# Float64 weights converted and split on VectorE, combinations 1024 columns at a time and in three phases

## The chip, the cores and the metric

The kernel runs on one core of a Trainium2 chip. The metric is the device time of one execution in microseconds (us); lower is better. The kernel before took 1769.65 us (median of three runs, 1762.01 to 1774.15).

## What is computed

Two attentions in a row for each of 8 batches and 8 heads (32 packed queries read 576 tokens; the tokens then read the packed result), and behind them two feed-forward layers over 4608 tokens, with 512 features at the ends and 2048 in the middle. All inputs come as 8-byte floats in the layout that the kernel reads as pairs of 32-bit words.

```python
def attn(q, k, v, p):
    packed = sm_attn(p, k, v)
    return sm_attn(q, packed, packed)
x = attn(q, k, v, p).transpose(0, 2, 1, 3).reshape(4608, 512)
h = x @ w_in                      # first up product
x = (h * cos(h)) @ w_out          # first down product
h = x @ w_in2                     # second up product
g = where(h >= 1, h, where(h <= -1, 0, (h + 1) ** 2 / 4))
out = g @ w_out2                  # second down product
```

## The kernel before, in words

Every operand of a large matmul is held as two parts, `hi` and `lo`, made by `split` (L66 to L69): ScalarE copies the source into the rounded `hi`, and another engine subtracts it from the source to give `lo`. Three matmuls (`TERMS`) stand for one product. That other engine is GpSimd unless a call names VectorE. The weights arrive as float64 and are made float32 by `convert` (L124 to L139): ScalarE scales the high words, VectorE does four integer and multiply operations (L131, L132, L135, L136), and GpSimd adds the two parts (L139).

The program runs in stages. Stage one is attention together with the first up product, where the attention's second half is folded into a matrix `M = packed @ w_in` per batch. A list of items `(n, hf, fp)` (L970 on) gives the order: batch `n`, half `hf` of its tokens, pair `fp` of feature tiles. `up` (L591) does 12 matmuls into `hps`, and `u`, a copy out of PSUM, goes to `h1T` in DRAM. Between two items, `step` advances side streams that are Python generators: `mat` and `load` make M (`form_M`, `load_M`: a product in `psB`, a copy `cp`, a turn through a DMA into `ml`, a split into `m`), `att` does attention, `wt` and `wo` convert weights. `cut_w_in` and `cut_w_out` make the weights of the first layer in 16 pieces of 128 x 512 each. `cut_w_out` is started at batch B - 2, and each item advances it by one step, two steps a piece; at `n == B - 1`, half 1, everything still open is drained in program order.

`combine` (L525) prepares the second layer's weights. The second up and down products use seven products in place of eight, in the manner of Strassen and Winograd, and so need sums of weight blocks. One unit converts four blocks of 128 x 256, two at a time, forms four sums, splits seven blocks in four calls (tile `pl`) and stores them to `su` or `sd` in DRAM. Eight units for the up weights run in stage one behind batch 2, eight for the down weights in the second up product.

Stage two, `run_down1`, is the first down product: 128 turns, each with 24 matmuls, an activation on ScalarE and VectorE (`act_a`, `act_b`) and a split into `r` on VectorE. Stage three, `run_up2`, is the second up product: seven products of 12 matmuls for each pair of feature tiles, their sums out of PSUM on VectorE (L708), an activation ending in L716, and the `ty` operands with differences and splits on GpSimd. `step("wt")` stands behind each product whose name does not begin with Z. Stage four, `run_down2`, is the second down product.

A tile scheduler sets the final order on each engine from program order, priorities and a model of times. `behind(last_act)` puts an instruction after the latest `u` copy of ScalarE.

## Time and profile before

| what | us |
|---|---|
| median of three runs | 1769.65 |
| lowest, highest | 1762.01, 1774.15 |
| the profiled execution | 1761.84 |
| its span, first to last instruction | 1759.9 |

Over the span TensorE is busy 90%, its weight loads 86%, VectorE 69%, ScalarE 53%, GpSimd 30%; the mean granted clock is 0.942 of full speed. In the profile, PE is TensorE, DVE VectorE, ACT ScalarE, POOL GpSimd. Matmuls are pipelined, so TensorE can count as busy without being at its rate; for that, matmul counts are set against time. The shares are averages over stages with different limits, so a stretch of the span is read by itself.

### The profile page before, as it was taken

Reading aid. Unit: us, or ns where it says so; the run is one execution under the profiler, and the core shown is the slowest. Engines: PE = TensorE matmul, PEld = TensorE weight load, DVE = VectorE, ACT = ScalarE, POOL = GpSimd, SP = SyncE. Lnnn points to the kernel's source line nnn. Section 1 sums busy time; section 2 is a strip of 40 time slices with the busy share of each in tenths; the row PEclk is TensorE's granted clock in tenths of the full one; section 3 lists DMA queues with packets and bytes.
Section 4 is the critical chain, followed back from the end, with each engine's and each line's share of the span. In section 5 each row is a group of like instructions: output and inputs, shape, how many; then the busy total and the mean of one; then the engine's idle time right before and its main releaser. Section 6 shows DMA issues by size and latency. Waiting matters only on the chain. (4 is left out here: it accounts for less than half of the span.)

```text
span 1759.9 us, 28596 instructions
## 1 busy us (share of the span) xinstructions
PE 1584.2 (90%) x10846; PEld 1514.2 (86%) x10846; DVE 1210.4 (69%) x1675; ACT 930.8 (53%) x1514; POOL 519.6 (30%) x376
## 2 busy tenths in 40 slices
PE   8679899897670999999999898998999899999998
PEld 6469688795560999999999888988999899999998
DVE  4883257455776887777776478888666597778775
ACT  3343344443333766666666367676766444444443
POOL 2863255565664010000001265556533000000000
PEclk7789799998975999999999999999999899999999
DMA  6566788988867444344342756565436954444430
GB/s 229 163 204 230 208 287 276 311 288 253 271 226 250 134 143 120 109 122 118 106 122 92 269 193 212 196 230 173 177 135 226 378 168 135 129 135 135 135 109 34
DMA packets 174538, 326.95 MB, mean 186 GB/s; under 512 B 16192, under 2 KB 70464, under 8 KB 170816
## 3 DMA queue, kind: packets, MB, share of 16 engines
q1 hardware_dynamic: 120128, 230.73, 42.6%
q10 hardware_dynamic: 54272, 94.39, 14.5%
q8 instruction: 85, 1.39, 0.3%
q14 instruction: 53, 0.43, 0.1%
HBM read 184.55 MB, written 130.02 MB: 179 GB/s over the span
## 5 line engine op out<-in xcount | busy, mean ns | idle before, releaser
L602 PE MATMUL hps<-at,m 128*128 128x288 f32 x1536 | 243.6, 313 | 42.1 <-ACT at L67 15.3
L602 PEld LDWEIGHTS hps<-at,m 128*128 128x128 f32 x1536 | 223.8, 199 | 59.0 <-ACT at L67 17.1
L67 ACT ACTIVATE r<-g 128x576 fp32r<-128x576 f32 x224 | 153.7, 687 | 184.6 <-PE psZ L909 72.6
L68 DVE TENSOR_TENSOR r<-g,r 128x576 fp32r<-128x576 f32 x224 | 166.3, 754 | 71.1 <-ACT r L67 71.1
L807 PE MATMUL psZ<-r,wo 128*128 128x288 f32 x1536 | 206.1, 296 | 0.0
L807 PEld LDWEIGHTS psZ<-r,wo 128*128 128x128 f32 x1536 | 205.2, 188 | 0.0
L68 POOL TENSOR_TENSOR ty<-td,ty 128x576 fp32r<-128x576 f32 x32 | 52.2, 1644 | 382.9 <-ACT ty L67 382.9
L68 DVE TENSOR_TENSOR r<-t,r 128x576 fp32r<-128x576 f32 x128 | 99.8, 779 | 95.0 <-ACT r L67 94.9
L909 PE MATMUL psZ<-r,sw 128*128 128x288 f32 x1152 | 159.6, 298 | 3.7 <-DVE r L68 2.8
L909 PEld LDWEIGHTS psZ<-r,sw 128*128 128x128 f32 x1152 | 156.5, 190 | 4.2 <-DVE r L68 3.0
L807 PE MATMUL psX<-r,wo 128*128 128x288 f32 x768 | 124.3, 297 | 37.9 <-ACT r L67 37.7
L716 DVE SCALAR_TENSOR_TENSOR t<-hh,t 128x576 f32<-128x576 f32 x128 | 123.9, 969 | 48.1 <-ACT t L715 48.0
L807 PEld LDWEIGHTS psX<-r,wo 128*128 128x128 f32 x768 | 110.1, 189 | 38.5 <-ACT r L67 38.0
L67 ACT ACTIVATE r<-t 128x576 fp32r<-128x576 f32 x128 | 87.8, 686 | 101.5 <-PE psZ L807 52.4
L714 ACT ACTIVATE t<-hh,half 128x576 f32<-128x576 f32 x128 | 98.5, 771 | 57.3 <-DVE hh L708 40.1
L807 PE MATMUL psY<-r,wo 128*128 128x288 f32 x768 | 123.9, 297 | 0.0
L730 PE MATMUL psZ<-ty,sw 128*128 128x288 f32 x768 | 113.9, 299 | 8.5 <-DVE hh L708 8.3
L730 PEld LDWEIGHTS psZ<-ty,sw 128*128 128x128 f32 x768 | 106.6, 190 | 10.1 <-DVE hh L708 9.8
L909 PE MATMUL psX<-r,sm 128*128 128x288 f32 x768 | 108.5, 301 | 7.3 <-ACT r L67 6.2
L909 PEld LDWEIGHTS psX<-r,sm 128*128 128x128 f32 x768 | 105.6, 192 | 8.5 <-ACT r L67 6.5
L807 PEld LDWEIGHTS psY<-r,wo 128*128 128x128 f32 x768 | 110.1, 189 | 0.0
L773 DVE SCALAR_TENSOR_TENSOR t<-h,t 128x576 f32<-128x576 f32 x128 | 99.0, 774 | 14.5 <-ACT t L772 5.4
(160 smaller groups left out, 3066.4 us busy)
## 6 DMA issues: line engine op xcount, KB each, us to landing
h1T<-u ACTq DMA_DIRECT2D x128, 288.0 KB, 3.5
h<-h1T SPq DMA_DIRECT2D x128, 288.0 KB, 2.8
gT<-t ACTq DMA_DIRECT2D x128, 288.0 KB, 2.3
g<-gT SPq DMA_DIRECT2D x128, 288.0 KB, 3.2
raw<-in_moe_w_in SPq DMA_DIRECT2D x32, 512.0 KB, 5.7
raw<-in_moe_w_out SPq DMA_DIRECT2D x32, 512.0 KB, 4.7
su<-pl SPq DMA_DIRECT2D x56, 256.0 KB, 4.4
sd<-pl SPq DMA_DIRECT2D x56, 256.0 KB, 3.0
```

The source lines that it names most:

```text
L67: nc.scalar.activation(out=hi, in_=src, func=AF.Copy)
L68: (eng or nc.gpsimd).tensor_tensor(out=lo, in0=src, in1=hi.bitcast(F32), op=ALU.subtract)
L602: nc.tensor.matmul(out=hps[:, j, :HB], lhsT=m[:, w, G, cs], rhs=x[:, G, y], start=(G == 0 and i == 0), stop=(G == 1 and i == 2),)
L714: nc.scalar.activation(out=t, in_=h, func=AF.Relu, scale=0.5, bias=half)
L716: nc.vector.scalar_tensor_tensor(out=t, in0=h, scalar=1.0, in1=t, op0=ALU.max, op1=ALU.min)
L730: nc.tensor.matmul(out=ps[:, i], lhsT=s[:, d, w, cs], rhs=t[:, d, y], start=first and d == n == 0, stop=d == 1 and n == 2, skip_group_chec ...
L773: nc.vector.scalar_tensor_tensor(out=t, in0=G1[i], scalar=1 / (2 * PI), in1=ki, op0=ALU.mult, op1=ALU.subtract)
L807: nc.tensor.matmul(out=acc[d // 2][:, d % 2], lhsT=wo[f // 4, w][:, f % 4, ds], rhs=r[:, y, k], start=f == n == 0, stop=f == NFT - 1 and n ...
L909: nc.tensor.matmul(out=ps[:, j], lhsT=s[:, f % 4, w, j * 128:j * 128 + 128], rhs=r[:, y, k], start=first and f == n == 0, stop=f == 7 and ...
```

## The change

`convert` adds its two parts on VectorE. All splits of weights (`w_in`, `w_out`, `pl`) and of M name VectorE. `cut_w_in` loads two pieces ahead, with three buffers. `combine` loads and converts a unit's four blocks in one piece of 1024 columns, puts the sums into the first half of the raw tile, and has no `slow`. Half of the down weights' units move into `run_down1`, one step every four turns, and are drained at turn 104; the other half stay in `run_up2`, where a step stands behind products X1 and X2 alone. `cut_w_out` starts half a batch (eight items) earlier. Splits and differences of attention (`at`, `mt`, `x`) and of `ty` stay on GpSimd.

```diff
@@ convert
-        nc.gpsimd.tensor_tensor(out=a, in0=a, in1=lf, op=ALU.add)
+        nc.vector.tensor_tensor(out=a, in0=a, in1=lf, op=ALU.add)
@@ cut_w_in (from_f64 and w_in_rows go)
+        def load(hp):
+            raw = stg.tile([128, 512, 2], I32, tag="raw", name="raw", bufs=3)
...
+        raws = [load(hp) for hp in range(2)]
+        for hp in range(4):
+            if hp % 2 == 0:
+                t = wpool.tile([128, 2, 2, 512], F32R, tag="w", name="wi")
+            a = stg.tile([128, 512], F32, tag="w32", name="w32", bufs=2)
+            convert(raws[hp], a)
+            if hp < 2:
+                raws.append(load(hp + 2))
+            yield
+            split(t[:, hp % 2, 0], t[:, hp % 2, 1], a, nc.vector)
@@ form_M, load_M, cut_w_out
-                split(t[:, 0, G], t[:, 1, G], a)
+                split(t[:, 0, G], t[:, 1, G], a, nc.vector)
...
-            split(t[:, 0, G], t[:, 1, G], halves[G])
+            split(t[:, 0, G], t[:, 1, G], halves[G], nc.vector)
...
-                split(wo[f // 4, 0][:, f % 4], wo[f // 4, 1][:, f % 4], a)
+                split(wo[f // 4, 0][:, f % 4], wo[f // 4, 1][:, f % 4], a, nc.vector)
@@ combine
-    def combine(units, slow):
-        def load(src, x):
-            raw = prep[0].tile([128, 2, 256, 2], I32, tag="raw", name="raw", bufs=2)
-            nc.sync.dma_start(out=raw, in_=src(x))
+    def combine(units):
+        def load(src):
+            raw = prep[0].tile([128, 4, 256, 2], I32, tag="raw", name="raw")
+            for x in range(2):
+                nc.sync.dma_start(out=raw[:, 2 * x:2 * x + 2], in_=src(x))
...
-            for raw, o in zip(raws, (slice(0, 4, 3), slice(1, 3))):
-                convert(raw, a[:, o], last_act)
-                yield
-                store()
-            s = prep[0].tile([128, 4, 256], F32, tag="raw", name="pc", bufs=2)
+            convert(raw, a, last_act)
+            store()
+            yield
+            s = raw[:, :2].bitcast(F32).rearrange("p m c t -> p (m c t)").rearrange("p (k c) -> p k c", c=256)
...
-                    split(hl[:, 0, :n], hl[:, 1, :n], x)
+                    split(hl[:, 0, :n], hl[:, 1, :n], x, nc.vector)
...
-                if k < 5:
-                    for _ in range(slow - 1):
-                        yield
...
+            if u + 1 < len(units):
+                raw = load(units[u + 1][0])
+                yield
@@ run_down1
+        prep[:] = [pd.enter_context(tc.tile_pool(name="prep1", bufs=1, reuse_waits="tile"))]
+        streams["wt"].append(combine(list(units_down())[:4]))
...
+            if i % 4 == 2:
+                step("wt")
             if i == 13 * 8:
+                drain("wt")
@@ run_up2
-        last_act.clear()
-        streams["wt"].append(combine(units_down(), 2))
+        streams["wt"].append(combine(list(units_down())[4:]))
...
-                    if o[0] != "Z":
+                    if o[0] == "X":
                         step("wt")
@@ items
-            streams["wt"].append(combine(units_up(), 2))
-        if n == B - 2 and fp == 0 and hf == 0:
+            streams["wt"].append(combine(units_up()))
+        if n == B - 3 and fp == 0 and hf == 1:
             streams["wo"].append(cut_w_out())
```

Line numbers move: L131 to L139 of before are L134 to L142 after, L609 is L604, L773 and L781 are L770 and L778.

The first place is VectorE at the end of stage one, from its last `u` copy on; `w` is a converted piece of `w_out`, `wo` its split tile. Before:

```order
L609 COPY u<-hps 128x576
L131 TENSOR_SCALAR w_4597<-raw 128x512
L132 SCALAR_TENSOR_TENSOR w_4597<-raw,w_4597 128x512
L135 TENSOR_SCALAR raw<-w_4597 128x512
L136 SCALAR_TENSOR_TENSOR raw<-raw 128x512
L131 TENSOR_SCALAR w_4610<-raw 128x512
L132 SCALAR_TENSOR_TENSOR w_4610<-raw,w_4610 128x512
L135 TENSOR_SCALAR raw<-w_4610 128x512
L136 SCALAR_TENSOR_TENSOR raw<-raw 128x512
L131 TENSOR_SCALAR w_4621<-raw 128x512
```

After:

```order
L604 COPY u<-hps 128x576
L68 TENSOR_TENSOR wo<-w_4461,wo 128x512
L134 TENSOR_SCALAR w_4509<-raw 128x512
L135 SCALAR_TENSOR_TENSOR w_4509<-raw,w_4509 128x512
L138 TENSOR_SCALAR raw<-w_4509 128x512
L139 SCALAR_TENSOR_TENSOR raw<-raw 128x512
L142 TENSOR_TENSOR w_4509<-w_4509,raw 128x512
L68 TENSOR_TENSOR wo<-w_4509,wo 128x512
L68 TENSOR_TENSOR pl<-raw,pl 128x512
L134 TENSOR_SCALAR w_4552<-raw 128x512
L135 SCALAR_TENSOR_TENSOR w_4552<-raw,w_4552 128x512
L138 TENSOR_SCALAR raw<-w_4552 128x512
```

Before, two conversions more follow these, then L773 of stage two, and their five splits stand on GpSimd. After, the rest of one conversion and two splits follow, then L770.

The second place is VectorE in the first turns of stage two, where `t` and `r` are the stage's own tiles and `h` its input. Before:

```order
L68 TENSOR_TENSOR r_4870<-t,r_4870 128x576
L773 SCALAR_TENSOR_TENSOR t<-h_4671,t 128x576
L68 TENSOR_TENSOR r_4904<-t,r_4904 128x576
L781 TENSOR_TENSOR t<-h_4669,t 128x576
L773 SCALAR_TENSOR_TENSOR t<-h_4673,t 128x576
L781 TENSOR_TENSOR t<-h_4671,t 128x576
L773 SCALAR_TENSOR_TENSOR t<-h_4834,t 128x576
L68 TENSOR_TENSOR r_4938<-t,r_4938 128x576
L781 TENSOR_TENSOR t<-h_4673,t 128x576
```

After:

```order
L778 TENSOR_TENSOR t<-h_4605,t 128x576
L134 TENSOR_SCALAR pa<-raw 128x1024
L770 SCALAR_TENSOR_TENSOR t<-h_4609,t 128x576
L778 TENSOR_TENSOR t<-h_4607,t 128x576
L135 SCALAR_TENSOR_TENSOR pa<-raw,pa 128x1024
L770 SCALAR_TENSOR_TENSOR t<-h_4773,t 128x576
L68 TENSOR_TENSOR r_4880<-t,r_4880 128x576
L778 TENSOR_TENSOR t<-h_4609,t 128x576
L138 TENSOR_SCALAR raw<-pa 128x1024
L68 TENSOR_TENSOR r_4914<-t,r_4914 128x576
L778 TENSOR_TENSOR t<-h_4773,t 128x576
```

The 1024-column operations on `pa` and `raw` are those of the first unit of `combine`; they now stand one by one between those of the stage.

The third place is where M is split, late in stage one: before, on GpSimd, where `m` is M's split tile, `ml` its source and `pl` that of `combine`.

```order
L68 TENSOR_TENSOR wo<-w_3913,wo 128x512
L68 TENSOR_TENSOR m<-ml,m 128x512 x3
L139 TENSOR_TENSOR pa<-pa,raw 128x2x256
L139 TENSOR_TENSOR w_4013<-w_4013,raw 128x512
L68 TENSOR_TENSOR m<-ml,m 128x512
L139 TENSOR_TENSOR pa<-pa,raw 128x512
L68 TENSOR_TENSOR m<-ml,m 128x512
L68 TENSOR_TENSOR wo<-w_4013,wo 128x512
L350 TENSOR_TENSOR x<-x,mx_4232 128x1152
L68 TENSOR_TENSOR m<-ml,m 128x512
L68 TENSOR_TENSOR pl<-pa,pl 128x512
```

After, on VectorE, in the same part of the program:

```order
L68 TENSOR_TENSOR m<-ml,m 128x512
L68 TENSOR_TENSOR wo<-w_3645,wo 128x512
L68 TENSOR_TENSOR wo<-w_3701,wo 128x512
L453 COPY cp<-psB 128x512
L134 TENSOR_SCALAR w_3772<-raw 128x512
L378 STREAM_TRANSPOSE a_3857<-x 128x576
L135 SCALAR_TENSOR_TENSOR w_3772<-raw,w_3772 128x512
L138 TENSOR_SCALAR raw<-w_3772 128x512
L139 SCALAR_TENSOR_TENSOR raw<-raw 128x512
L142 TENSOR_TENSOR w_3772<-w_3772,raw 128x512
L134 TENSOR_SCALAR pa<-raw 128x1024
L68 TENSOR_TENSOR wo<-w_3772,wo 128x512
```

The splits of M have moved into the queue in which `cp`, the copies out of `psB`, and the conversions stand.

## Rows read from the trace of the kernel before

**Rows 1.** The table of stretches, all engines; columns named in its first line
```profile
core 0: us, PE busy (x) PEld busy (x) DVE busy (x) ACT busy (x) POOL busy (x), PEclk, DMA share, GB/s
0.00:130.00 130.00, 97.10 (x399) 75.81 (x400) 90.03 (x131) 53.88 (x114) 78.04 (x63) 0.76 0.63 198
130.00:400.00 270.00, 249.31 (x1520) 220.04 (x1518) 136.07 (x232) 112.40 (x238) 124.78 (x100) 0.96 0.81 266
400.00:533.00 133.00, 89.17 (x482) 77.85 (x481) 89.40 (x113) 49.70 (x85) 85.06 (x63) 0.83 0.80 258
533.00:570.60 37.60, 0.02 (x1) 0.02 (x1) 25.27 (x32) 14.72 (x23) 18.53 (x14) 0.55 0.66 228
570.60:982.20 411.60, 411.37 (x3072) 411.02 (x3073) 291.77 (x394) 268.90 (x399) 17.48 (x11) 1.00 0.43 128
982.20:1226.90 244.70, 219.34 (x1539) 213.50 (x1537) 197.35 (x253) 158.31 (x252) 140.80 (x91) 0.96 0.60 203
1226.90:1366.30 139.40, 139.40 (x1046) 139.40 (x1047) 93.28 (x118) 99.24 (x151) 54.88 (x34) 1.00 0.49 183
1366.30:1417.00 50.70, 40.66 (x268) 39.17 (x267) 32.02 (x47) 24.71 (x38) 0.00 (x0) 0.87 0.89 346
```

**Rows 2.** TensorE's timeline: start us, us, instruction, count [idle before, releaser]
```profile
488.47 1.09 PE L602 MATMUL hps<-at,m 128*128 128x288 f32 x3 [14.13 <-ACT at L67]
...
531.00 1.88 PE L602 MATMUL hps<-at,m 128*128 128x288 f32 x12 [2.05 <-ACT u L611]
570.58 0.61 PE L807 MATMUL psX<-r,wo 128*128 128x288 f32 x1 [37.70 <-ACT r L67]
...
956.60 25.76 PE L807 MATMUL psZ<-r,wo 128*128 128x288 f32 x192
```

**Rows 3.** VectorE's timeline, 440 to 580, the same columns
```profile
471.38 2.35 DVE L552 TENSOR_TENSOR pc<-pa 128x256 f32<-128x256 f32 x1
...
508.28 0.41 DVE L552 TENSOR_TENSOR pc<-pa 128x256 f32<-128x256 f32 x1
...
543.93 0.69 DVE L132 SCALAR_TENSOR_TENSOR w<-raw,w 128x512 int32<-128x512 int32 x1
544.66 0.43 DVE L135 TENSOR_SCALAR raw<-w 128x512 int32<-128x512 int32 x1
...
548.23 1.37 DVE L135 TENSOR_SCALAR raw<-w 128x512 int32<-128x512 int32 x1
```

**Rows 4.** GpSimd's timeline, 500 to 580, the same columns
```profile
537.86 1.39 POOL L68 TENSOR_TENSOR wo<-w,wo 128x512 fp32r<-128x512 f32 x1 [0.74 <-ACT wo L67]
...
547.92 1.39 POOL L68 TENSOR_TENSOR wo<-w,wo 128x512 fp32r<-128x512 f32 x1 [0.74 <-ACT wo L67]
...
562.40 1.26 POOL L68 TENSOR_TENSOR wo<-w,wo 128x512 fp32r<-128x512 f32 x1 [0.74 <-ACT wo L67]
```

**Rows 5.** ScalarE's timeline, 455 to 580; ACTq is its queue of issues
```profile
472.47 8.20 ACTq L86 DMA_DIRECT2D h1T<-u  x2
480.77 0.65 ACT L611 ACTIVATE u<-hps 128x576 f32<-128x576 f32 x1 [8.33 <-DVE u L609]
...
561.70 0.63 ACT L67 ACTIVATE wo<-w 128x512 fp32r<-128x512 f32 x1 [3.40 <-POOL w L139]
564.65 1.41 ACT L772 ACTIVATE t<-h 128x576 int32<-128x576 f32 x2 [2.32 <-DMA h<-h1T]
```

**Rows 6.** Groups by line and shape, whole span: busy us, mean ns, idle before, releasers
```profile
L716 DVE SCALAR_TENSOR_TENSOR t<-hh,t 128x576 f32<-128x576 f32 x128 | 123.9, 969 | 48.1 <-ACT t L715 48.0
...
L68 DVE TENSOR_TENSOR r<-t,r 128x576 fp32r<-128x576 f32 x128 | 99.8, 779 | 95.0 <-ACT r L67 94.9
L773 DVE SCALAR_TENSOR_TENSOR t<-h,t 128x576 f32<-128x576 f32 x128 | 99.0, 774 | 14.5 <-ACT t L772 5.4
...
L68 POOL TENSOR_TENSOR m<-ml,m 128x512 fp32r<-128x512 f32 x64 | 87.2, 1373 | 67.0 <-ACT m L67 52.8 <-DVE x L343 4.9 <-DMA raw<-in_moe_w_out 3.9
```

**Rows 7.** Who TensorE waited for, 0 to 533: total us, times, longest us
```profile
PE psB L449 <- ACT cp L455: 20.3, 12, 4.8
```

More of the change, by code (lines that the diff above doesn't have):

```diff
@@ L122, in drain, with words @@
             pass
+    def words(src):
+        return src.bitcast(I32)
     def convert(raw, a, after=()):
@@ L391, in new_M @@
         ready.add(("new", n, c))
-    def from_f64(src, dst):
-        raw = stg.tile([128, 512, 2], I32, tag="raw", name="raw", bufs=2)
-        nc.sync.dma_start(out=raw, in_=words(src).rearrange("p (c t) -> p c t", t=2))
-        a = stg.tile([128, 512], F32, tag="w32", name="w32", bufs=2)
-        convert(raw, a)
-        yield
-        split(dst[:, 0], dst[:, 1], a)
-    def w_in_rows(c, hp):
-        return w_in[hp * 128:(hp + 1) * 128, c * 512:(c + 1) * 512]
     WI = {}
     def cut_w_in(c):
-        for i in range(2):
-            t = wpool.tile([128, 2, 2, 512], F32R, tag="w", name="wi")
-            for j in range(2):
-                yield from from_f64(w_in_rows(c, 2 * i + j), t[:, j])
-                WI[c, 2 * i + j] = t[:, j]
-                ready.add(("wi", c, 2 * i + j))
-                yield
+        def load(hp):
+            raw = stg.tile([128, 512, 2], I32, tag="raw", name="raw", bufs=3)
+            src = words(w_in[hp * 128:(hp + 1) * 128, c * 512:(c + 1) * 512])
+            nc.sync.dma_start(out=raw, in_=src.rearrange("p (c t) -> p c t", t=2))
+            return raw
+        raws = [load(hp) for hp in range(2)]
[8 more added lines that the diff above has]
+            split(t[:, hp % 2, 0], t[:, hp % 2, 1], a, nc.vector)
+            WI[c, hp] = t[:, hp % 2]
+            ready.add(("wi", c, hp))
+            yield
     def form_M(g, c):
@@ L538, in combine @@
         units = list(units)
-        raws = [load(units[0][0], x) for x in range(2)]
+        raw = load(units[0][0])
         yield
         for u, (_, dst) in enumerate(units):
-            following = units[u + 1][0] if u + 1 < len(units) else None
             a = prep[0].tile([128, 4, 256], F32, tag="pa", name="pa")
-            for raw, o in zip(raws, (slice(0, 4, 3), slice(1, 3))):
-                convert(raw, a[:, o], last_act)
-                yield
-                store()
-            s = prep[0].tile([128, 4, 256], F32, tag="raw", name="pc", bufs=2)
-            raws = [load(following, 0)] if following else []
+            convert(raw, a, last_act)
+            store()
+            yield
+            s = raw[:, :2].bitcast(F32).rearrange("p m c t -> p (m c t)").rearrange("p (k c) -> p k c", c=256)
             tt = nc.vector.tensor_tensor
-            tt(out=s[:, 0], in0=a[:, 3], in1=a[:, 2], op=ALU.add)
-            tt(out=s[:, 2], in0=a[:, 0], in1=a[:, 3], op=ALU.subtract)
+            tt(out=s[:, 0], in0=a[:, 1], in1=a[:, 3], op=ALU.add)
+            tt(out=s[:, 2], in0=a[:, 0], in1=a[:, 1], op=ALU.subtract)
             tt(out=s[:, 1], in0=s[:, 0], in1=a[:, 0], op=ALU.subtract)
-            tt(out=s[:, 3], in0=a[:, 1], in1=s[:, 1], op=ALU.subtract)
+            tt(out=s[:, 3], in0=a[:, 2], in1=s[:, 1], op=ALU.subtract)
             yield
@@ L557, in combine @@
                 hl = prep[0].tile([128, 2, 2, 256], F32R, tag="pl", name="pl")
[L558 removed]
+                x = {0: a[:, 0:4:2], 2: a[:, 3:4], 3: s[:, :2], 5: s[:, 2:]}[k]
                 with behind(last_act):
[L560 removed]
+                    split(hl[:, 0, :n], hl[:, 1, :n], x, nc.vector)
                 for i in range(n):
@@ L564, in combine @@
                 store()
-                if k < 5:
-                    for _ in range(slow - 1):
-                        yield
-            if following:
-                raws.append(load(following, 1))
-            yield
-        store()
+            if u + 1 < len(units):
+                raw = load(units[u + 1][0])
+                yield
     def units_up():
```

3 lines of the change are left out of this document (removed).

## Prediction

> **What bounds the kernel now.** Read the table of stretches first [rows 1], then TensorE's timeline for the places where it stands still [rows 2], then what VectorE, GpSimd and ScalarE do there [rows 3 to 5], then the groups by line [rows 6]. In the table the reader is to compare matmul counts with time. At full rate TensorE runs 192 matmuls in 25.76 us [rows 2], that is 0.1333 us each.
>
> Four stages. (a) Attention and the first up product end at 570.6, where the first L807 matmul starts after 37.70 us of idleness [rows 2]. (b) The first down product, 570.6 to 982.2: 3072 x 0.1333 = 409.6 of 411.6 us, so TensorE alone sets it. (c) The second up product: 1539 x 0.1333 = 205.2 of 244.7 us up to 1226.9, 39.5 lost; then 1046 x 0.1333 = 139.4 of 139.4, nothing lost. The lossy part is the part in which combine runs. (d) The handover to the second down product, 1366.3 to 1417: 268 matmuls, 35.7 of 50.7 us, 15 lost [rows 1]. Stage (a) is far from the rate nearly everywhere: TensorE is busy 97.1 of 130 us at a mean clock of 0.76, 249.3 of 270, and 89.2 of 133 at 0.83, which mixes 2.4 and 1.2 GHz [rows 1]. No engine is full there; chains are what lasts: a result goes from ScalarE to GpSimd or from VectorE to GpSimd and back before a weight can be used.
>
> A second thing is to be seen in rows 3 and 4. The same VectorE operation has two prices. L135 takes 0.43 us at 544.66, with GpSimd idle, and 1.37 at 548.23, beside GpSimd's 1.39 us split at 547.92. L552 takes 0.41 at 508.28 and 2.35 at 471.38. In the groups L716 has a mean of 969 ns, L773, the same shape in a stage with hardly any GpSimd work, 774 [rows 6]. So work that leaves GpSimd also makes VectorE's own work shorter.
>
> **The change, part by part.** Prices on VectorE alone: 0.41 us for 256 columns, 0.69 for 512 with two inputs, 0.43 for 512 with one [rows 3]. From 0.41 and 0.69 each further 256 columns cost 0.28, so 1024 columns are estimated at 1.25; the one-input form at 0.86 at most.
>
> Load of VectorE in stage (a). Added: 64 splits of M, 32 splits and 32 sums of weights, 512 columns each, 128 x 0.69 = 88 us; for eight units of combine a sum of 1.25, three splits of 0.69 and one of 0.41, 8 x 3.7 = 30. It is busy 90.0 + 136.1 + 89.4 + 25.3 = 341 of 570.6 us now [rows 1]. 341 + 118 = 459 is 80%, before anything is given back by GpSimd falling silent. So it does not become the bound on average.
>
> (1) End of stage (a). After TensorE's last first-up matmul (531.00 + 1.88) six w_out tiles are still split on GpSimd, at 537.86 to 562.40, 4.9 us apart ((562.40 - 537.86) / 5) [rows 4]; then ScalarE has its last wo at 561.70, waits for h1 until 564.65 [rows 5], and the first matmul comes at 570.58. In the order of the changed kernel the stream starts eight items earlier and behind the last u copy stand three splits and two conversions, where four conversions (five splits) stood. Two tiles less: 2 x 4.9 = 9.8. The other three lose a GpSimd sum and split of about 1.39 each [rows 4] for 0.69 each on VectorE: 3 x 1.4 = 4.2, and one transfer between engines each. I take -15. Bounds: -28 (37.70 less the 8.9 us from the last wo to the first matmul, which nothing here removes) and +5 (VectorE's three splits wait for ScalarE one by one).
>
> (2) The chain to the last batch. At 488.47 TensorE has waited 14.13 us for the split attention of the last batch [rows 2]. ScalarE stood for 8.20 us at the issue of an h1T store that needs a u copy of VectorE [rows 5], and VectorE's work in front of that copy was stretched, as L552 with 2.35 us for 0.41 [rows 3]. I take half of the 14.13, -7; bounds -14 and +10 (this stretch now holds more VectorE work).
>
> (3) Start and M. A split of M on GpSimd takes 1373 ns on the mean [rows 6], on VectorE 0.69. TensorE's largest wait up to 533 is 20.3 us on ScalarE's copies out of psB [rows 7]; that in-order engine holds splits that wait for GpSimd's sums. I take half, -10; bounds -30 (the same gain in the other waits of the start) and +15.
>
> (4) Second up product. A unit of combine has eleven steps now, four steps per pair of feature tiles, and such a pair takes TensorE 84 x 0.1333 = 11.2 us: 88 / 4 x 11.2 = 246 us, as the table has it. Four units of seven steps at two per pair take 28 / 2 x 11.2 = 157 us. At the same loss per us (39.5 / 244.7) that is 25.3, a gain of 14. GpSimd loses all its sums and splits of combine there and keeps those of ty, so VectorE's L716 (969 against 774 ns) gets part of its time back. I take -18; bounds 0 and -36.
>
> Here a rule bears on the size. The Trainium skill, "SBUF — State Buffer", section "SBUF: two separate sides", has VectorE and GpSimd share one pair of ports as an exclusive lock, for the whole instruction, against VectorE operations with two SBUF inputs among others. By it the loss of (4) would shrink with GpSimd's busy time as well as with the number of units, and (4) would lie beyond 18. The trace agrees as far as L716 goes, and shows L135, with one input, stretched too; no run here has the stage without GpSimd.
>
> (5) First down product. Four units come in: two conversions of 0.86 and three of 1.25, four combinations of 0.41, splits of 2.48, together 9.6 us a unit, 38 us. VectorE is idle for 411.6 - 291.8 = 120 us there [rows 1], 94.9 of them before r splits because ScalarE's r is not there yet [rows 6], and TensorE is never short of r. The scheduler puts one long operation between two or three of the stage's own. What is queued behind it is the next r; a unit is spread over 28 turns of 3.2 us, so the cover holds. I take +1; bounds 0 and +10.
>
> (6) Handover (d): g, its stores and the sd loads are as they were: 0, bounds -5 and +5.
>
> Sum: -15 - 7 - 10 - 18 + 1 = -49. The profiled execution took 1761.84 us (span 1759.9), so 1713. It lies 8 us below the median shown, 1769.65; 1% of that median, 18 us, is about what a measurement here can tell from no change.
>
> **Rivals.** The end is set elsewhere. Stage (a) keeps its pace because transfers do: DMA is 0.81 busy in 130 to 400 and 0.80 in 400 to 533 [rows 1], and each w_out tile also waits for its 512 KB. Then only the two tiles of (1) go, 10 us, and (4) yields 5: 1747. For it: the DMA share. Against it: TensorE's waits name ScalarE and VectorE.
>
> VectorE holds up what stands behind a split. GpSimd idled 67.0 us before its M splits, 52.8 of them for ScalarE's m [rows 6], and nobody stood behind it. On VectorE the u and psB copies stand behind, and TensorE waits for those. If all 67 land on TensorE and (1) and (3) bring nothing, the sum is 67 - 7 - 18 + 1 = +43: 1805. It decides from about 67 - 49 = 18 us too much, i.e. if more than 49 us of that idleness comes over. Against it: VectorE has other work in the order between two M splits, and 20% of slack.
>
> That rival has a page behind it. The Trainium skill, "TensorE: Matmul & The Clock Gate", section "Architectural detail: the array is 16× 32×32, not 1× 128×128", calls the ScalarE and VectorE queues strictly first in, first out. ScalarE's 8.20 us behind one store [rows 5] agree; the page by itself makes the time longer, by as much as the rival says.
>
> More than I count. The waits of stage (a) outside (1) and (2) shrink as a whole, (3) reaching its bound of -30, and (1) comes to -23: 1713 - 20 - 8 = 1685.
>
> That the change does not do what it says can be left out: the order of the changed kernel has GpSimd with 149 instructions for 373.
>
> **How the numbers follow.** Forecast 0.57, its own range 1690 to 1742; elsewhere 0.18; VectorE holds up 0.11; more than counted 0.14. The range goes from 1675, a little beyond the 1685 case, to 1770, which takes in 1747 and leaves out the slower rival. Faster by over 1% is below 1752: 0.57 + 0.14 and a little over a third of the second case, 0.78. Slower by over 1% (above 1787): 0.10. Within: 0.12.
>
> **What would show it.** The first L807 matmul starts near 539 (570.6 - 32) after an idle time near 23 us; VectorE's 512-column operations in stage (a) come near 0.43 and 0.69 on the mean; stage (b) is still 410 to 413 us long; the second up product loses near 22 us, within its first 160. It is wrong if TensorE's waits before 533 name VectorE with more than 49 us, if stage (b) has gaps, or if the first L807 stays beyond 560.

## The result and the profile after

The changed kernel takes 1748.33 us (median of eight runs), the kernel before 1763.96 in its eight: ratio 0.9907, 95% interval 0.9882 to 0.9933. That is a gain of 15.6 us where 49 were forecast. The profiled execution took 1746.79 us. First the table of stretches, with the same columns as [rows 1] and cut at the same events.

```profile
0.00:130.00 130.00, 93.54 (x368) 70.66 (x369) 97.97 (x180) 55.89 (x117) 21.49 (x22) 0.75 0.67 202
130.00:400.00 270.00, 243.06 (x1419) 214.25 (x1418) 140.95 (x245) 105.51 (x217) 36.56 (x30) 0.91 0.75 246
400.00:533.00 133.00, 102.30 (x570) 88.12 (x569) 112.69 (x178) 56.42 (x95) 17.89 (x12) 0.83 0.84 268
533.00:571.40 38.40, 7.99 (x47) 7.50 (x45) 23.76 (x41) 13.82 (x22) 0.00 (x0) 0.63 0.88 328
571.40:985.20 413.80, 412.59 (x3071) 411.77 (x3072) 318.61 (x446) 276.58 (x419) 17.63 (x11) 0.99 0.51 154
985.20:1212.40 227.20, 210.05 (x1540) 205.57 (x1539) 169.37 (x214) 150.25 (x230) 77.62 (x47) 1.00 0.51 177
1352.00:1402.00 50.00, 37.88 (x268) 36.85 (x266) 31.37 (x46) 25.50 (x39) 0.00 (x0) 0.90 0.92 352
```

Read it against [rows 1] by stage. Stage (a) ends at 571.4, where it ended at 570.6: nothing gained. Stage (b) is 2.2 us longer (413.8 for 411.6). The lossy part of stage (c) is 17.5 us shorter (227.2 for 244.7). The handover (d) has its 268 matmuls in 50.0 us for 50.7. So the whole gain of this pair of profiles is stage (c)'s. Now TensorE's timeline at the end of stage (a), to be set beside [rows 2].

```profile
510.67 1.09 PE L597 MATMUL hps<-at,m 128*128 128x288 f32 x3 [9.23 <-ACT at L67]
...
539.07 5.00 PE L597 MATMUL hps<-at,m 128*128 128x288 f32 x24 [3.07 <-ACT u L606]
571.42 0.61 PE L804 MATMUL psX<-r,wo 128*128 128x288 f32 x1 [27.36 <-ACT r L67]
```

The first matmuls of the first up product, before and after:

```profile
66.75 0.85 PE L602 MATMUL hps<-at,m 128*128 128x288 f32 x2 [0.85 <-ACT at L67]
```

```profile
73.03 0.85 PE L597 MATMUL hps<-at,m 128*128 128x288 f32 x2 [0.48 <-ACT at L67]
```

The idle time before the first down product fell from 37.70 to 27.36 us and the wait for the last batch from 14.13 to 9.23. But the last first-up matmul now ends near 544, where it ended near 533, and that eats both. Who TensorE waited for up to 533, first before, then after (total us, times, longest):

```profile
PE psB L449 <- DVE cp L453: 7.9, 9, 2.6
```

```profile
PE psB L449 <- DVE cp L453: 16.2, 10, 3.5
PE psB L449 <- ACT cp L455: 15.7, 13, 3.3
PE hps L597 <- ACT at L67: 11.5, 5, 9.2
PE hps L597 <- ACT m L67: 11.1, 9, 4.1
PE psA L278 <- DMA vraw<-in_v: 8.0, 3, 4.7
```

The wait for ScalarE's `cp` shrank [rows 7: 20.3]; that for VectorE's `cp` doubled, and one for v's load is new. The group of stage three that answers to [rows 6]:

```profile
L711 DVE SCALAR_TENSOR_TENSOR t<-hh,t 128x576 f32<-128x576 f32 x128 | 114.8, 898 | 49.3 <-ACT t L710 49.2
```

969 ns (L716 in the kernel before) became 898; the same shape in the stage with hardly any GpSimd work had 774.

### The profile page after: what moved, and what is told of

Its sections match the earlier page's. It is cut to its first block, busy times and chain, and to the rows that moved or that the text cites. A ratio compares the mean times of both kernels' runs of the same rounds, so it can differ in the third digit from the quotient of the medians.

```text
span 1745.0 us, 28350 instructions
## 1 busy us (share of the span) xinstructions
PE 1584.8 (91%) x10846; PEld 1511.3 (87%) x10846; DVE 1236.8 (71%) x1819; ACT 927.2 (53%) x1498; POOL 220.7 (13%) x152
## 5 line engine op out<-in xcount | busy, mean ns | idle before, releaser
L597 PE MATMUL hps<-at,m 128*128 128x288 f32 x1536 | 249.4, 320 | 30.7 <-ACT at L67 11.5
L597 PEld LDWEIGHTS hps<-at,m 128*128 128x128 f32 x1536 | 229.9, 205 | 47.3 <-ACT m L67 16.1
L711 DVE SCALAR_TENSOR_TENSOR t<-hh,t 128x576 f32<-128x576 f32 x128 | 114.8, 898 | 49.3 <-ACT t L710 49.2
L449 PE MATMUL psB<-wi,mt 128*128 128x512 f32 x192 | 76.1, 512 | 36.3 <-DVE cp L453 16.2
```

What stands on the lines that cost most here:

```text
L449: nc.tensor.matmul(out=ps, lhsT=x[:, hp], rhs=w[:, y], start=(i == 0), stop=(i == 2))
L597: nc.tensor.matmul(out=hps[:, j, :HB], lhsT=m[:, w, G, cs], rhs=x[:, G, y], start=(G == 0 and i == 0), stop=(G == 1 and i == 2),)
L711: nc.vector.scalar_tensor_tensor(out=t, in0=h, scalar=1.0, in1=t, op0=ALU.max, op1=ALU.min)
```

## Experiments

All kernels in one table. Ratios are against the kernel before, run beside each; the rows come from several chips, on which the kernel before had 1763.64 to 1767.26 us, so small differences between medians of two rows are read by their ratios. The last three columns come from one profile each: start of the first down matmul; from there to the start of the last; first to 1537th matmul of the second up product.

| kernel | median us | ratio (95%) | (a) ends | (b) | (c) |
|---|---|---|---|---|---|
| before | 1763.96 | 1 | 570.6 | 411.5 | 244.7 |
| changed | 1748.33 | 0.9907 (0.9882 to 0.9933) | 571.4 | 413.8 | 227.0 |
| 1 M on GpSimd | 1750.74 | 0.9918 (0.9891 to 0.9945) | 574.5 | 417.9 | 228.8 |
| 2 w_out late | 1755.59 | 0.9950 (0.9933 to 0.9967) | 578.7 | 415.6 | 226.8 |
| 3 w_in on GpSimd | 1750.71 | 0.9921 (0.9898 to 0.9945) | 571.4 | 419.1 | 227.0 |
| 4 second layer only | 1752.91 | 0.9933 (0.9908 to 0.9958) | 573.2 | 414.4 | 233.7 |
| 5 old up units | 1765.87 | 1.0015 (1.0000 to 1.0030) | 590.4 | 412.6 | 227.6 |
| 6 old w_in loads | 1761.41 | 0.9986 (0.9970 to 1.0003) | 571.8 | 418.9 | 234.5 |
| 7 w_out on GpSimd | 1754.30 | 0.9935 (0.9913 to 0.9957) | 570.1 | 416.4 | 226.0 |
| 8 no spread | 1764.39 | 0.9996 (0.9982 to 1.0010) | 571.4 | 412.1 | 238.7 |
| 9 two moved | 1743.45 | 0.9874 (0.9849 to 0.9900) | 569.3 | 414.2 | 224.3 |
| 10 four moved | 1736.38 | 0.9841 (0.9813 to 0.9869) | 549.2 | 418.4 | 228.2 |
| 11 cp first | 1753.25 | 0.9940 (0.9918 to 0.9962) | 571.4 | 418.2 | 226.1 |
| 12 four moved, w_out on GpSimd | 1745.82 | 0.9890 (0.9866 to 0.9914) | 564.9 | 419.7 | 230.0 |
| 13 four moved, r first | 1733.67 | 0.9819 (0.9792 to 0.9846) | 553.1 | 421.9 | 229.8 |
| 14 four moved, old engines | 1725.33 | 0.9783 (0.9760 to 0.9807) | 542.4 | 419.2 | 229.9 |
| 15 six moved, r first | 1718.24 | 0.9737 (0.9712 to 0.9762) | 528.2 | 422.5 | 227.9 |
| 16 as 13, M on GpSimd | 1729.06 | 0.9797 (0.9775 to 0.9820) | 549.2 | 417.2 | 225.7 |
| 17 six moved, old engines | 1723.29 | 0.9772 (0.9742 to 0.9802) | 535.0 | 424.8 | 228.4 |
| 18 as 17, w_out early | 1722.66 | 0.9754 (0.9725 to 0.9782) | 532.9 | 425.9 | 229.6 |

### Where the gain is: 4 and 8

Run 4 gives the kernel before the changed kernel's units of the down weights and nothing else (`combine2` is the changed `combine`; `combine` stays for the up weights).

```diff
@@ run_down1
...
+        streams["wt"].append(combine2(list(units_down())[:4]))
...
+            if i % 4 == 2:
+                step("wt")
...
@@ run_up2
...
-        streams["wt"].append(combine(units_down(), 2))
+        streams["wt"].append(combine2(list(units_down())[4:]))
...
-                    if o[0] != "Z":
+                    if o[0] == "X":
```

> The kernel before, with the change in the down weights' units alone (1024 columns at a time, four of them in the first down product, VectorE for their sums and splits); stage one is the one of before. Theory: all of the gain comes from the second up product, and the first stage of the changed kernel brings nothing. Then the second up product takes 227 us for its first 1536 matmuls as in the changed kernel (244.7 before), stage one ends at 570 within 3, and the time is that of the changed kernel or up to 5 us below it, 1743 to 1749. Rival: the second up product gains only because it starts with other clock or buffers from stage one; then it stays near 240 us, and the time is near 1760.

Run 8 keeps the changed kernel, without the four units in stage (b).

```diff
@@ run_down1
...
-        streams["wt"].append(combine(list(units_down())[:4]))
@@ run_up2
-        streams["wt"].append(combine(list(units_down())[4:]))
+        streams["wt"].append(combine(units_down()))
```

> The changed kernel, with all eight units of the down weights in the second up product, at the changed pace of two steps per pair of feature tiles; none in the first down product. Term 4 had the loss of the second up product go with the number of units' steps (39.5 us over 246 us before, about 22 over 157 us in the changed kernel). If that holds, eight units lose twice as much as four: the whole product is 18 to 24 us longer, the first down product 2 to 3 us shorter, and the time is 1763 to 1770. Rival 'price' (the loss came from GpSimd's part and from the narrow operations, so it is gone wherever the units run): 3 to 8 us longer, 1750 to 1756.

Run 4 has two thirds of the gain (1752.91, above the range expected); its interval overlaps the changed kernel's. Its (c), 233.7, lies between the 227 of the theory and the 240 of the rival: the code is the changed kernel's, but the order of instructions there is another one, and the granted clock of that stretch is 0.96, where the changed kernel has 1.00. Which of the two costs the 7 us is not shown. Run 8 has no gain. Its stretches:

```profile
571.40:983.50 412.10, 411.87 (x3072) 411.52 (x3073) 291.72 (x394) 268.97 (x399) 17.46 (x11) 0.99 0.42 128
983.60:1222.30 238.70, 214.65 (x1538) 208.27 (x1537) 183.30 (x230) 151.81 (x235) 78.26 (x47) 0.98 0.54 184
1222.30:1392.00 169.70, 164.36 (x1202) 162.75 (x1201) 130.73 (x170) 116.95 (x179) 48.59 (x30) 0.98 0.63 232
```

The second up product takes 408.4 us (983.6 to 1392.0) for the changed kernel's 387.4, so four more units cost it 21 us, and stage (b) gets 1.7 back. That is what term 4 built on: the loss goes with the number of units, about 5 us each in (c) and under 1 in (b). Without the spread everything else together is worth nothing (0.9996). By these profiles the second up product itself was not shortened by the engine or the width of the operations: measured in the same way, from the first to the last of its matmuls, it took 403.5 us in the kernel before (982.2 to 1385.7) with its eight units on GpSimd, and takes 408.4 in run 8 with eight on VectorE.

### One part of stage (a) undone: 1, 2, 3, 5, 6, 7, 11

```diff
@@ run 1, form_M (load_M likewise)
-                split(t[:, 0, G], t[:, 1, G], a, nc.vector)
+                split(t[:, 0, G], t[:, 1, G], a)
```

> The changed kernel, with the splits of M alone back on GpSimd. In the changed kernel the last first-up matmul ends 11 us later than before, and TensorE's waits for VectorE's cp in front of L449 are 16.2 us (7.9 before). Theory 'queue' (VectorE's one queue now puts splits of M and weights in front of the copies that TensorE waits for): the waits for VectorE's cp fall to near 8 us, the last first-up matmul comes 5 to 11 us earlier than 543.8, and the time falls to 1738 to 1743. Rival 'early start' (it is w_out starting eight items earlier that delays the items): no change there, 1748 within 3. Rival 'more is better' (M on GpSimd is the slower way, as term 3 had it): 5 to 10 us later, 1753 to 1758.

```diff
@@ run 11, form_M: both copies stand under it
+                with tc.high_priority(offset=PRI_MAIN):
                     if s:
                         nc.vector.tensor_copy(out=t, in_=ps)
...
```

> The changed kernel, with the copies cp out of psB, on both engines, put at the raised priority that the u copies have, so that the scheduler places them ahead of splits and conversions; the work is the same. Theory 'queue': TensorE's waits for VectorE's cp fall from 16.2 to under 8 us and for ScalarE's from 15.7 to under 10, the last first-up matmul comes 3 to 10 us before 543.8, and the time is 1740 to 1748. Rival 'chain' (the copies are late because their product is late, not because of what stands ahead of them): waits and time as in the changed kernel, 1748 within 3.

The same wait in run 1 and in run 11:

```profile
PE psB L449 <- DVE cp L453: 17.2, 10, 5.3
```

```profile
PE psB L449 <- DVE cp L454: 15.9, 9, 3.4
```

It is 16.2 in the changed kernel. Taking M's splits off VectorE leaves it there, so M's splits alone are not what the copies stand behind; raising the copies' priority leaves it there too, and neither time can be told from 1748.33. But run 11 does not settle for the rival that the copies are late because their product is late, since the raised priority did not put them first. One product and its copy in run 11, TensorE and then VectorE:

```profile
446.62 0.97 PE L449 MATMUL psB<-wi,mt 128*128 128x512 f32 x3 [1.18 <-ACT cp L456]
```

```profile
448.08 0.69 DVE L142 TENSOR_TENSOR w<-w,raw 128x512 f32<-128x512 f32 x1
448.69 0.69 DVE L68 TENSOR_TENSOR m<-ml,m 128x512 fp32r<-128x512 f32 x1
449.29 0.69 DVE L135 SCALAR_TENSOR_TENSOR w<-raw,w 128x512 int32<-128x512 int32 x1
...
450.56 0.69 DVE L454 COPY cp<-psB 128x512 f32<-128x512 f32 x1
```

The product is there at 447.59, and the copy comes 2.97 us later, behind conversions, splits and sums. Over VectorE's 32 copies `cp`, the mean time from the end of the product to the start of the copy is 0.60 us in the kernel before, 1.14 in the changed kernel, 1.42 in run 1 and 1.00 in run 11. In the five kernels with the old stage (a) it is 0.41 to 0.60, in the other fifteen 0.77 to 1.42. So the copies do stand behind more work on VectorE than before, of which M's splits are only a part; what that costs at the end of the stage these runs do not show.

```diff
@@ run 2, items
-        if n == B - 3 and fp == 0 and hf == 1:
+        if n == B - 2 and fp == 0 and hf == 0:
```

> The changed kernel, with cut_w_out started where it was before (batch B - 2, half 0). Theory 'early start': the items between 350 and 530 us run up to 11 us earlier than in the changed kernel, but two more w_out tiles are left behind the last item, so that the first down matmul comes within 3 us of 571.4, and the time stays near 1748. Theory 'queue': the items gain 3 us or less, the idle time before the first down matmul grows from 27.4 to about 34 us, and the time rises by 4 to 8 us, to 1752 to 1756.

```diff
@@ run 7, cut_w_out; convert takes the engine of its sum as an argument
-            convert(raw, a, last_act)
+            convert(raw, a, last_act, nc.gpsimd)
...
-                split(wo[f // 4, 0][:, f % 4], wo[f // 4, 1][:, f % 4], a, nc.vector)
+                split(wo[f // 4, 0][:, f % 4], wo[f // 4, 1][:, f % 4], a)
```

> The changed kernel, with the sums and splits of w_out alone back on GpSimd; the early start stays. Term 1 put three tiles left behind the last item at 1.4 us each less, 4.2 us, and the rest of its gain into the earlier start. By it the idle time before the first down matmul grows from 27.4 to about 32 us and the time to 1752 within 3. Theory 'queue': with 32 operations fewer on VectorE between 430 and 540 us the items come 5 to 10 us earlier, the idle time grows by as much, and the time stays at 1748 or falls by up to 5.

Run 2 brings the idle time back to 37.61 us, with the last first-up matmul 3 us earlier, and costs 7.3 us of time, so the early start is worth that much. Run 7 is 6 us slower by its median, near what term 1 said, though the intervals overlap. Its profile (its fastest execution, 1746.88) shows another holder of the end. ScalarE, and VectorE at the same time:

```profile
562.28 0.61 ACT L67 ACTIVATE pl<-raw 128x512 fp32r<-128x512 f32 x1
568.81 0.63 ACT L67 ACTIVATE pl<-raw 128x512 fp32r<-128x512 f32 x1 [5.91 <-DMA su<-pl]
569.35 2.40 ACT L67 ACTIVATE r<-t 128x576 fp32r<-128x576 f32 x4
```

```profile
561.18 2.09 DVE L778 TENSOR_TENSOR t<-h,t 128x576 f32<-128x576 f32 x3
```

r's inputs are there at 563.3 (561.18 + 2.09), and r comes at 569.35, because the last unit's split stands in front of it and waits for the store of the one `pl` buffer. The Trainium skill, "TensorE: Matmul & The Clock Gate", section "Architectural detail: the array is 16× 32×32, not 1× 128×128", has ScalarE's queue strictly first in, first out; this row agrees.

```diff
@@ run 3, cut_w_in; convert takes the engine of its sum as an argument
-            convert(raws[hp], a)
+            convert(raws[hp], a, add=nc.gpsimd)
...
-            split(t[:, hp % 2, 0], t[:, hp % 2, 1], a, nc.vector)
+            split(t[:, hp % 2, 0], t[:, hp % 2, 1], a)
```

> The changed kernel, with the sum and the split of w_in alone back on GpSimd (loading stays two pieces ahead). In the changed kernel the first first-up matmul comes at 73.0 us, 6.3 later than before. Theory 'queue': the w_in work on VectorE stands in front of the copies and transposes of the first attention; the first first-up matmul comes back to 67 to 69 us, and 0 to 6 us of that reach the end of the stage: 1742 to 1748. Rival 'loading' (the new order of loads delays the loads of the first attention): still near 73, and 1748 within 3.

```diff
@@ run 6, cut_w_in
-            raw = stg.tile([128, 512, 2], I32, tag="raw", name="raw", bufs=3)
+            raw = stg.tile([128, 512, 2], I32, tag="raw", name="raw", bufs=2)
...
-        raws = [load(hp) for hp in range(2)]
...
+            raw = load(hp)
...
-            convert(raws[hp], a)
-            if hp < 2:
-                raws.append(load(hp + 2))
+            convert(raw, a)
```

> The changed kernel, with the pieces of w_in loaded as before, each where it is converted, with two buffers; sum and split stay on VectorE. Theory 'loading' (two pieces loaded ahead put 1 MB in front of the loads of the first attention, and later of v): the first first-up matmul goes from 73 to 62 to 68 us, as in the two runs with the old loading, the waits for v's rows (8.0 us) go, and the time falls by 3 to 8 us, to 1740 to 1745. Rival 'engine': the first first-up matmul stays at 72 to 76, and the time at 1748 within 3.

```diff
@@ run 5, items; combine_old is the combine of before, sums and splits on GpSimd
-            streams["wt"].append(combine(units_up()))
+            streams["wt"].append(combine_old(units_up(), 2))
```

> The changed kernel, with combine for the up weights alone as it was before (512 columns at a time, eleven steps a unit, sums and splits on GpSimd). In the changed kernel the first-up matmuls fall behind those of before from the 832nd on, 14 to 31 us at the 960th to the 1280th, while these units run. Theory 'long operations' (operations of 1024 columns at one step an item stand in VectorE's queue in front of the copies for TensorE): the lag at the 1280th goes from 31 to under 15 us, the stage ends 5 to 12 us earlier, and the time is 1736 to 1744. Rival 'whole load' (it is the sum of everything on VectorE, no part by itself): the lag stays over 20 us, and the time is 1745 to 1752.

Run 3: engine of w_in, no difference (first first-up matmul at 76.1). Runs 5 and 6 missed every expectation, 17 and 13 us slower than the changed kernel. Run 5 ends (a) 19 us later, with a wait of 23.16 us for the last batch. Run 6 starts earlier (69.6 for 73.0) and ends (a) the same, and then loses 5 us in (b) and 7 in (c), whose code is the changed kernel's: the order of instructions there is another one too, and the granted clock in (c) is 0.96 for 1.00, so these 12 us need not come from w_in's loads. Why the parts, each undone, cost 2 to 17 us while all of stage (a) undone together (run 4) costs 4.6 is not shown by these runs. Effects of single edits do not add up here.

### Units out of stage (a): 9, 10, 12, 13, 15

```diff
@@ items; N is 6 in run 9, 4 in run 10
-            streams["wt"].append(combine(units_up()))
+            streams["wt"].append(combine(list(units_up())[:N]))
@@ run_down1
-        streams["wt"].append(combine(list(units_down())[:4]))
+        streams["wt"].append(combine(list(units_up())[N:] + list(units_down())[:4]))
...
-            if i % 4 == 2:
+            if i % 2 == 0:
```

> The changed kernel, with the last two of the eight units of the up weights moved out of stage one into the first down product, ahead of its four down units; there a step stands behind every second turn. Theory 'units end the stage' (one unit takes about 40 us by its chain of single buffers, the eighth is split at 531 to 560 us in the changed kernel, and the first operands r stand behind it on ScalarE, as in the run with w_out on GpSimd, where r was held 6 us by the last split): stage one ends 6 to 14 us earlier, at 557 to 565, the first down product is 0 to 2 us longer, the time 1735 to 1743. Rival 'transfers' (the loads of w_out and the stores of h1T set the end whatever the units do): the stage ends at 568 to 573, and the time is 1746 to 1751.

> The same with four of the eight units of the up weights moved into the first down product. Theory 'units end the stage': once the units end well before the last item, moving more of them helps only through the queues: 1733 to 1743, within 5 us of the run with two moved, and the first down product is 1 to 4 us longer. Rival 'whole load' (each unit's 10 us on VectorE costs wherever TensorE waits on VectorE): each unit moved gains 2 to 4 us, so this run is 4 to 8 us below the run with two moved.

Run 12 adds the edit of run 7 to run 10.

> Four units moved, and the sums and splits of w_out on GpSimd. With w_out on GpSimd alone the items ended 4 us earlier, but r was held by the last unit's split. Theory 'units end the stage': that hold is gone, so the stage ends at 555 to 563 and the time is within 4 us of the run with four units moved and w_out on VectorE. Theory of term 1 (three tiles at 1.4 us each dearer on GpSimd, behind the last item): 4 to 8 us above that run.

Run 9 is 5 us faster by its median than the changed kernel, run 10 is 12 faster: (a) ends 22 us earlier, and (b) is 4.6 longer. Run 9 missed both of its ranges: its time lies between them, and its (a) ends at 569.3, where the rival "transfers" had it. The 7 us from run 9 to run 10 speak for the rival in which each unit's load costs, though the intervals of the two runs overlap. Run 12 is 9 us slower than run 10, a little more than term 1 would have it. Both 9 and 10 show a new wait at the handover. ScalarE in run 10, and SyncE's issue of the load that it waits for:

```profile
538.27 2.77 ACT L777 ACTIVATE t<-t,halfpi 128x576 f32<-128x576 f32 x4
547.40 1.13 ACT L132 ACTIVATE raw<-raw 128x1024 f32<-128x1024 f32 x1 [6.36 <-DMA raw<-in_moe_w_in]
548.44 2.39 ACT L67 ACTIVATE r<-t 128x576 fp32r<-128x576 f32 x4
```

```profile
539.39 1.26 SPq L529 DMA_DIRECT2D raw<-in_moe_w_in  x2
```

r's inputs are there at 541.0 (538.27 + 2.77 on ScalarE; VectorE's products end 0.8 later), and r comes at 548.44, because the first moved unit's conversion was put ahead of it and waits for its load. Run 13 ties the conversion behind the fourth r; run 15 does so with six units moved.

```diff
@@ runs 13 (N is 4) and 15 (N is 2, and i % 4 != 3), run_down1, against run 10
...
                 hi = nc.scalar.activation(out=r[:, 0], in_=t, func=AF.Copy)
...
+                if i == 3:
+                    last_act[:] = [hi.ins]
...
-            if i % 2 == 0:
+            if i >= 8 and i % 2 == 0:
```

> Four of the up weights' units moved into the first down product, the steps there from turn 8 on, and the first unit's conversion placed behind the fourth r on ScalarE. In the run without this, r's inputs were there at 541 us, and r came at 548.4, behind a conversion that waited for its load. If that is all, the first down matmul comes 6 to 8 us earlier, at 541 to 544, and the time is 1728 to 1732 (5 to 8 below 1736.4). Rival: the load is late in any case, and later turns stand behind it: the first down product is longer by as much, and the time stays at 1736.

> As the run with four moved and r first, with six of the eight units moved. If each unit costs stage one 3 us by its load on VectorE, the stage ends 4 to 8 us earlier than with four and the first down product is 1 to 3 us longer: 1724 to 1730. If the units in the second half of the stage (the last four) were the ones that cost, nothing is gained: 1729 to 1734.

ScalarE in run 13:

```profile
549.66 2.77 ACT L777 ACTIVATE t<-t,halfpi 128x576 f32<-128x576 f32 x4
552.34 2.40 ACT L784 ACTIVATE r<-t 128x576 fp32r<-128x576 f32 x4
558.92 1.15 ACT L132 ACTIVATE raw<-raw 128x1024 f32<-128x1024 f32 x1 [4.19 <-DMA raw<-in_moe_w_in]
```

r follows at once, and TensorE's idle time in front of the first down product falls from 23.09 to 16.41 us, as expected. (b) is 3.5 longer, so half goes back, as the rival had it; the medians (1736.38, 1733.67) can't be told apart. (That run 13's (a) ends later than run 10's is no effect of the edit: see the last section.) Run 15 is better than expected: 1718.24 us, 2.6% below the kernel before and the lowest median of all, with (a) ending 43 us earlier than in the changed kernel. Its stage (b) takes ten units:

```profile
528.20:950.80 422.60, 415.58 (x3073) 411.74 (x3074) 358.36 (x522) 286.87 (x447) 18.03 (x11) 1.00 0.65 202
```

VectorE is busy 358 of 423 us, and TensorE loses 8.8 us against the changed kernel's 413.8: about 1.5 for each unit moved.

What in a unit costs stage (a) these runs don't tell apart. A moved unit takes its work on VectorE and ScalarE out of the stage, and with it two loads of 512 KB and seven stores of 256 KB. The transfers up to the end of stage (a), in the changed kernel and in run 15:

```profile
DMA packets 78113, 140.81 MB, mean 247 GB/s; under 512 B 7531, under 2 KB 31083, under 8 KB 77308
```

```profile
DMA packets 62979, 117.72 MB, mean 223 GB/s; under 512 B 6592, under 2 KB 19392, under 8 KB 62944
```

Transfers alone do not set the end: at 247 GB/s the 23.1 MB less would be 94 us by estimate, and 43 were gained, at a lower rate. That they hold the stage in part is not excluded.

### The engine: 14, 16, 17, 18

Runs 14 and 17 are run 4 with four and six units of the up weights moved and r first; all else in stage (a) is the kernel before. Run 18 starts w_out early as well; run 16 is run 13 with run 1's edit.

```diff
@@ run 14 against run 4, items and run_down1 (run 17: 2 for 4; r first as in run 13)
-            streams["wt"].append(combine(units_up(), 2))
+            streams["wt"].append(combine(list(units_up())[:4], 2))
...
-        streams["wt"].append(combine2(list(units_down())[:4]))
+        streams["wt"].append(combine2(list(units_up())[4:] + list(units_down())[:4]))
...
```

> The kernel before with the down weights' units as in the changed kernel, and with four units of the up weights (the other four as before) moved into the first down product like the run with r first; w_in, w_out, M and the other four units stay on GpSimd and are started as before. Theory 'load' (what costs is the units' work in stage one, on whichever engine): the stage ends 10 to 20 us earlier than 570.6 and the time is 1735 to 1745. Theory 'engine' (VectorE in place of GpSimd shortens the chains of stage one as terms 1 to 3 had it): the stage stays above 562 us, and the time is 1748 to 1756, some 20 us above the run with four moved and r first.

> As the run with four moved and the old engines, with six of the eight units of the up weights moved. Theory 'GpSimd is the better place' (stage one's splits and sums beside VectorE's queue): some 8 us below the run with six moved on VectorE again, 1708 to 1713. Theory 'engine is indifferent' (the pair before differed by its order): 1715 to 1721.

> The same, with w_out started eight items earlier as in the changed kernel, its sums and splits still on GpSimd. By the run with the late start (7 us on VectorE) the idle time before the first down matmul falls and the time is 4 to 9 us below the run with six moved and the old engines. Rival: the w_out stream then stands in front of the items' copies, and the items are later by as much: within 3 us of it.

> As the run with four moved and r first, with the splits of M back on GpSimd. Theory 'queue' (splits of M stand in front of TensorE's copies, which matters where VectorE is full): with VectorE at less load the difference is within 3 us either way. Term 3 (GpSimd's 1373 ns against 0.69 us in a chain): 4 to 10 us slower than that run.

Three pairs, VectorE's stage (a) against GpSimd's: no unit moved 0.9907 and 0.9933, four 0.9819 and 0.9783, six 0.9737 and 0.9772. All intervals overlap, and the sign changes. Moving four units gains 15 to 28 us with either set of engines; the set makes no difference that five to eight executions of each can show. Run 14 is 10 us below the lower of its two ranges, run 17 lies 2 above the higher of its own. In run 18 TensorE's idle time before (b) falls from 26.91 to 16.45 us, and the time stays: its rival was right, the last first-up matmul is 8 us later. Run 16 is 4.6 us below run 13, on the other side of term 3, outside both of its ranges, and its interval overlaps run 13's.

## Why the prediction was wrong, step by step

- Term 4 (second up product, -18): its number was right, -17.5, and run 8 shows the larger part of it, the 14 us for fewer units: four units cost 21 us. That it came so close is in part luck: the eighteen profiles with four units there have 224.3 to 234.5 us in (c), a gain of 10 to 20. The smaller part, VectorE relieved of GpSimd, shows in durations but not in time, since run 8 has that relief and its second up product is 5 us longer than before. L716's 969 ns fell to 898 as GpSimd's busy time there halved (140.80 to 77.62 us). The Trainium skill, "SBUF — State Buffer", section "SBUF: two separate sides", has the two engines share ports as an exclusive lock: the durations agree, but the stage did not gain more than 18, as the prediction had worked out from that page.
- Term 5 (+1): +2.2. Term 6 (0): -0.7. Both right.
- Term 1 (-15): the idle time fell by 10.3, and run 2 shows 7 us of time in the early start. Mis-sized by a third, and then given back: the last first-up matmul was 11 us later.
- Term 2 (-7): the wait fell by 4.9; given back.
- Term 3 (-10): this step failed. It took half of the wait for ScalarE's `cp` (it fell by 4.6) and set nothing against it in the sum. The wait for VectorE's `cp` rose by 8.3, v's load added 8.0, and the first first-up matmul came at 73.0 us for 66.7; all runs with the old w_in code start at 61.9 to 66.7, and those with the new loads at 72.1 to 76.1.
- The sum: -32 for stage (a), measured +0.8; the first down matmul at 571.4 is the prediction's own sign of being wrong, "beyond 560". Three local gains were added as if each came off the end of the stage, and the costs in other places of the stage (the start, `cp`, v's load, the clock from 130 to 400 us: 0.91 for 0.96) were not priced at all. How these costs share the 33 us is not shown. The load estimate was not what failed: VectorE is busy 375 of 571 us there (97.97 + 140.95 + 112.69 + 23.76), under the 459 that I allowed.
- The rivals: "the end is set elsewhere" had the time, 1747, by another sum (10 from term 1, 5 from term 4); that transfers hold the stage is neither shown nor excluded, since moving a unit, which moved the end by 22 and 43 us, moves its transfers too, and the engine sets, which load the same bytes, came out alike. "VectorE holds up" had the mechanism in part: the copies `cp` on VectorE stand behind other work longer than before (1.14 us for 0.60 on the mean), and TensorE's wait for them doubled. It had not the size, and M's splits alone don't decide.

What I did not see: the same spread that made term 4 right was open to the up weights' units, and is worth 30 us more (run 15).

## What to carry to other kernels

Preparation work has a price that depends on the stage it stands in: here, by single profiles, one unit cost about 5 us in the second up product, 5 to 8 of stage (a)'s end where four or six were moved, and 0.2 to 2 where TensorE runs at rate on operands made ahead. Try moving it there before changing its engine. In a stage without a full engine, don't add up gains of single waits; what the end does when work is taken out tells more than who is waited for.

## What the runs showed of the hardware that was not expected

One order of instructions gives different clocks. Runs 10 and 13 have the same order on every engine up to the first r. Their profiles from 130 to 400 us, 10 and then 13:

```profile
130.00:400.00 270.00, 243.74 (x1468) 214.58 (x1468) 140.11 (x245) 104.84 (x221) 36.60 (x31) 0.94 0.76 249
```

```profile
130.00:400.00 270.00, 242.70 (x1404) 214.16 (x1403) 137.82 (x240) 103.37 (x214) 36.71 (x30) 0.89 0.74 241
```

TensorE is as busy, and does 64 matmuls fewer at a granted clock of 0.89 for 0.94; the last first-up matmul starts at 536.3 for 525.6. So the end of (a) in a single profile carries some 10 us that no edit made (run 4 and the kernel before, one order too, differ by 2.6 in it, run 8 and the changed kernel by nothing). Differences of 20 us and more, and medians, are what the verdicts on stage (a) rest on.

With that in mind, the changed kernel loses in stage (a) by TensorE's clock too. The stretch from 200 to 400 us, before and after:

```profile
200.00:400.00 200.00, 184.63 (x1143) 161.98 (x1142) 113.53 (x192) 90.86 (x191) 104.45 (x83) 0.99 0.86 282
```

```profile
200.00:400.00 200.00, 180.29 (x1021) 156.76 (x1020) 118.41 (x205) 86.15 (x176) 27.67 (x23) 0.91 0.81 262
```

TensorE is busy only 4.3 us less, but does 122 matmuls fewer, as its granted clock has a mean of 0.91 for 0.99 between its levels of 1.2 and 2.4 GHz. One such place of the changed kernel:

```profile
271.85 0.66 PE L257 MATMUL psA<-ident,s 128*128 128x128 f32 x4 [0.65 <-ACT pt L287]
272.92 1.03 PE L597 MATMUL hps<-at,m 128*128 128x288 f32 x3 [0.42 <-ACT at L67]
273.75 0.41 PE L257 MATMUL psA<-ident,s 128*64 128x128 f32 x1
274.56 7.03 PE L597 MATMUL hps<-at,m 128*128 128x288 f32 x33 [0.39 <-POOL at L68]
```

and the same group in the kernel before:

```profile
270.75 4.64 PE L602 MATMUL hps<-at,m 128*128 128x288 f32 x33
```

Three waits of 0.65, 0.42 and 0.39 us, among short transposes, stand ahead of 33 matmuls that take 7.03 us for 4.64, at a mean granted clock of 0.62:

```profile
274.50:281.60 7.10, 7.04 (x34) 7.05 (x35) 2.51 (x4) 2.48 (x3) 2.10 (x3) 0.62 0.75 239
```

No view of waits shows these 2.4 us; the granted clock does. It is not this pair alone: from 130 to 400 us the five kernels with the old stage (a) (before, 4, 14, 17, 18) have 0.94 to 0.96, the fifteen others 0.89 to 0.94. That short waits bring the clock down is not shown: from 130 to 400 us TensorE has 30 idle times under 1 us in run 10, 14.3 us together, at a clock of 0.94, and 20 in run 13, 8.1 us together, at 0.89. Why the new stage (a) runs at the lower clock was not tried.

On VectorE the wide operations cost what was estimated: 0.69 us for 1024 columns with one input and 1.22 with two (0.86 at most and 1.25).

```profile
442.55 0.69 DVE L138 TENSOR_SCALAR raw<-pa 128x1024 int32<-128x1024 int32 x1
443.75 1.22 DVE L139 SCALAR_TENSOR_TENSOR raw<-raw 128x1024 f32<-128x1024 uint32 x1
```
